# Out's weight combinations on another engine and in pieces, block fetches ahead of loads, x scaled one product later, last output on two queues

## The chip, the cores and the metric

The kernel runs on one core of one Trainium2 chip. The metric is the device time of one execution in microseconds (us), as a median over the runs that lie in the fast state. The kernel before takes 1222.24 us (1219.61 to 1223.46, three runs). "Faster" or "slower" needs a difference of over 2%.

Engine names in the profile: PE is TensorE's matmul side and PEld its weight loading, DVE is VectorE, ACT is ScalarE, POOL is GpSimd, SP is SyncE. A name with a "q" behind it (SPq, ACTq) is the engine's sequencer, which issues DMA transfers.

## The reference, cut to what matters

```python
# q, k, v: (8 batches, 8 heads, 576 positions, 64), fp32
scores = q @ k.T / sqrt(64) * Dmat[h]        # Dmat: gamma[h]**(i-j) for i >= j, else 0
attn = scores @ v                            # -> x: (4608 tokens, 512)
xn = x / sqrt(mean(x*x) + 1e-6) * rms_g
g, val = xn @ w_gate, xn @ w_val             # 512 -> 1536
out = (silu(g) * val) @ w_out                # 1536 -> 512
```

All is fp32.

## The kernel before

The 4608 tokens are cut into 12 blocks u of 384. Blocks 0 and 1 are computed with plain products. Blocks 2 to 11 use a scheme with 7 products of half-size quarters in place of 8, in the manner of Strassen. It needs sums of the quarters of the weights and of x.

- **Up stages.** Each block has six stages i = 0 to 5, alternately for the gate and for the value. A stage has seven products in the order x y z x w z w (these letters are the PSUM banks they write), of 8 matmuls and 1.30 us each.
- **Out.** Then come seven products xo zo wo yo xo zo wo of 24 matmuls and 3.90 us each. Product k reads a block of combined weights in slot k % 4 of the tile `w_out`. The seven blocks lie in DRAM (`w_blocks`, 768 KB each), because only four fit.
- **Attention slots.** Between stages stands the attention work for a later block: many small 64x64 matmuls, then transposes and scalings on DVE and ACT, then the loads for the next but one.

The combination of the weights for Out, which happens once, and its fetches:

```python
def keep(blk, t):
    nc.sync.dma_start(out=w_blocks[blk], in_=t)

def combine_out():
    a11, a12, a21, a22 = (quarter(r, c) for r in range(2) for c in range(2))
    for o, a, b, op in (
        (a22, a21, a22, ALU.add), (a21, a11, a21, ALU.subtract),
        (a11, a22, a11, ALU.subtract), (a12, a12, a11, ALU.subtract),
    ):
        nc.gpsimd.tensor_tensor(out=o, in0=a, in1=b, op=op)      # 128 x 6 x 256
    return (S1, a22), (S3, a21), (S2, a11), (S4, a12)

def fetch():
    nonlocal n_fetched
    if n_fetched < 7 * (NU - 2):
        nc.sync.dma_start(
            out=w_slots[:, n_fetched % 4], in_=w_blocks[ORDER[n_fetched % 7]])
        n_fetched += 1

def across(u):                                 # Out of block u
    ...
    def product(rhs, ps, start):
        k = 7 * (u - 2) + n_done
        ...                                    # 24 matmuls with w_slots[:, k % 4]
        fetch()                                # refills the slot just read
    ...
    def result(row, col, a, ps):
        ...                                    # add, transpose into o
        for d in range(2):
            for i in range(P // SQ):
                nc.sync.dma_start(out=out[...], in_=o[i * SQ : i * SQ + SQ, d])
```

The order of the work. `slot` is the attention work, `following` prepares the next slot and issues loads (13 of them) for the one after it, and `norm_2` scales the next block's x and forms the sums of its quarters (the four instructions `L412`):

```python
def following(j):
    if j + 1 < len(jobs):
        prepare(j + 1)                         # two DVE transposes, four ACT scalings
    if j + 2 < len(jobs):
        load_qk(j + 2)
        load_kv(j + 2)

SLOTS = (((0, 2, 4, 5), 5), ((5,), 9), ((1, 3, 5), 10))    # stages with a slot, by u % 3

def behind(u, i):
    at, n = SLOTS[u % 3]
    if i in at:
        j = u // 3 * 8 + n + at.index(i)
        slot(j)
        following(j)
    if u + 1 < NU and i >= 5:
        (norm_0, norm_1, norm_2)[i - 5](u + 1)

kept = start()                                 # blocks 0 and 1; ends with combine_out()
for u in range(2, NU):
    for i in range(2 * NG):
        for _ in up(u, i % 2, i // 2):
            pass
        if u == 2 and i == 2:
            for blk, t in kept:
                keep(blk, t)
            for _ in range(4):
                fetch()
        if i == 2 * NG - 1:
            rest = across(u)
            next(rest)
        behind(u, i)
    for i, _ in enumerate(rest):               # after each product of Out
        if i in (1, 3):
            behind(u, 6 + i // 2)
```

## Time and profile before

| | before |
|---|---|
| time, median of 3 runs | 1222.24 us |
| span of the profiled run | 1222.0 us |
| PE busy | 1150.0 us, 94% |
| DVE busy | 676.9 us, 55% |
| DMA fetches of weight blocks | 70 of 768 KB |

The waits view lists, for TensorE, what it stood waiting for. Its columns are engine, tile and line, what released the wait, then microseconds in total, the number of waits and the longest. For the kernel before, from 280 us to the end, beside the wait of xo:

```profile
PE y L432 <- DVE sums L412: 8.1, 1, 8.1
...
PE z L432 <- DVE sum L282: 4.0, 1, 4.0
PE ms L379 <- DVE sq L372: 1.4, 7, 0.2
PE wo L557 <- DVE h L568: 0.5, 2, 0.2
```

A single wait of 8.1 us and one of 4.0 stand beside small ones that recur. From 280 us on, such a list, with the half clock that follows some of the waits and the tail after the last matmul, is nearly the whole inventory of what a change to the order of the work can win.

### The profile page before, as it was taken

What the parts mean: (1) busy time and instruction counts of PE and PEld (TensorE: products, weight loads), DVE (VectorE), ACT (ScalarE), POOL (GpSimd) and SP (SyncE); (2) the same over time, 40 slices, a digit from 0 to 9 for tenths busy, and PEclk for the clock granted to TensorE, in tenths of its full rate; (3) what the DMA queues carried; (4) which work ended last, traced back from release to release, by engine and by line L of the source; (5) the groups of instructions that cost most, each with busy time, mean ns of one, the idle gap of its engine ahead of it and who ended that gap; (6) DMA issues with size and microseconds to landing.
All of it is one profiled execution on the core that took longest, in us unless ns stands there. A gap on an engine that the chain in (4) does not pass through costs nothing.

```text
span 1222.0 us, 24026 instructions
## 1 busy us (share of the span) xinstructions
PE 1150.0 (94%) x10184; PEld 1036.6 (85%) x10184; DVE 676.9 (55%) x1346; ACT 244.1 (20%) x468; POOL 59.7 (5%) x78
## 2 busy tenths in 40 slices
PE   4697899996999999999999999999999999999997
PEld 3555555444998999999998999999999999999997
DVE  3888871027565567446556557437557555436352
ACT  4454550010220121120120121120120120110110
POOL 0000004134000000000000000000000000000000
PEclk9798799997999999999999999999999999999999
DMA  8588431020386426306335526405345503404203
GB/s 220 120 207 206 125 119 52 18 64 14 73 246 180 104 44 181 98 1 177 84 62 150 134 40 162 121 1 151 97 76 148 137 2 105 103 1 143 65 4 101
DMA packets 302347, 126.28 MB, mean 103 GB/s; under 512 B 279328, under 2 KB 284832, under 8 KB 302240
## 3 DMA queue, kind: packets, MB, share of 16 engines
q1 hardware_dynamic: 293168, 105.70, 35.2%
q10 hardware_dynamic: 9072, 19.05, 4.8%
q8 instruction: 80, 1.31, 0.5%
q14 instruction: 27, 0.22, 0.1%
HBM read 109.75 MB, written 14.94 MB: 102 GB/s over the span
## 4 chain that ended last, share of the span: by engine, by line
PE 74%; DVE 9%; DMA 3%; SPq 1%; issue 1%; ACT 0%; DVEq 0%; POOL 0%; POOLq 0%
PE x L432 13%; PE z L432 13%; PE w L432 13%; PE y L432 6%; PE up L489 6%; PE wo L557 6%; PE out L503 5%; PE xo L557 4%; PE zo L557 4%; DMA w_out<-w_blocks 3%; DVE sum L282 1%; PE av L318 1%; DVE h L568 1%; PE yo L557 1%; DVE sums L412 1%; PE av L299 1%
## 5 line engine op out<-in xcount | busy, mean ns | idle before, releaser
L456 ACT COPY m<-x 128x384 f32<-128x384 f32 x60 | 28.7, 478 | 439.4 <-PE x L432 439.4
L432 PE MATMUL z<-x,w_gate 128*128 128x192 f32 x480 | 89.3, 330 | 4.0 <-DVE sum L282 4.0
L557 PE MATMUL xo<-h,w_out 128*128 128x192 f32 x480 | 84.3, 333 | 6.8 <-DMA w_out<-w_blocks 6.8
L557 PEld LDWEIGHTS xo<-h,w_out 128*128 128x128 f32 x480 | 79.5, 193 | 12.0 <-issue 10.9
L432 PE MATMUL x<-x,w_gate 128*128 128x192 f32 x480 | 89.3, 329 | 0.0
L432 PE MATMUL x<-x,w_val 128*128 128x192 f32 x480 | 88.8, 328 | 0.0
L432 PE MATMUL z<-x,w_val 128*128 128x192 f32 x480 | 87.8, 326 | 0.0
L432 PE MATMUL w<-sums,w_val 128*128 128x192 f32 x480 | 87.8, 326 | 0.0
L432 PE MATMUL w<-sums,w_gate 128*128 128x192 f32 x480 | 87.8, 326 | 0.0
L432 PEld LDWEIGHTS z<-x,w_gate 128*128 128x128 f32 x480 | 80.7, 192 | 4.5 <-DVE sum L282 4.5
L557 PE MATMUL wo<-h,w_out 128*128 128x192 f32 x480 | 82.3, 328 | 0.5 <-DVE h L568 0.5
L432 PEld LDWEIGHTS x<-x,w_gate 128*128 128x128 f32 x480 | 80.1, 192 | 0.5
L432 PEld LDWEIGHTS x<-x,w_val 128*128 128x128 f32 x480 | 79.2, 190 | 0.6
L432 PEld LDWEIGHTS w<-sums,w_val 128*128 128x128 f32 x480 | 79.7, 190 | 0.0
L432 PEld LDWEIGHTS w<-sums,w_gate 128*128 128x128 f32 x480 | 79.7, 190 | 0.0
L432 PEld LDWEIGHTS z<-x,w_val 128*128 128x128 f32 x480 | 79.6, 190 | 0.0
L557 PEld LDWEIGHTS wo<-h,w_out 128*128 128x128 f32 x480 | 77.9, 190 | 1.1 <-DVE h L568 1.1
L439 DVE TENSOR_TENSOR u<-m,y 128x384 f32<-128x384 f32 x60 | 32.6, 543 | 80.0 <-PE y L432 77.8
L439 DVE TENSOR_TENSOR h<-u,w 128x384 f32<-128x384 f32 x60 | 33.2, 554 | 78.2 <-PE w L432 78.2
L489 PE MATMUL up<-x,w_gate 128*128 128x384 f32 x192 | 67.7, 512 | 3.7 <-DVE x L401 1.8
L489 PEld LDWEIGHTS up<-x,w_gate 128*128 128x128 f32 x192 | 37.9, 200 | 32.6 <-issue 4.9
L489 PE MATMUL up<-x,w_val 128*128 128x384 f32 x192 | 65.0, 499 | 0.0
(120 smaller groups left out, 1759.9 us busy)
## 6 DMA issues: line engine op xcount, KB each, us to landing
w_out<-w_blocks SPq DMA_DIRECT2D x70, 768.0 KB, 4.9
k<-in_k_dram SPq DMA_DIRECT2D x64, 128.0 KB, 2.9
v<-in_v_dram SPq DMA_DIRECT2D x64, 128.0 KB, 2.9
qraw<-in_q_dram SPq DMA_DIRECT2D x112, 72.0 KB, 2.5
kraw<-in_k_dram SPq DMA_DIRECT2D x112, 72.0 KB, 2.6
out_dram<-o SPq DMA_DIRECT2D x320, 24.0 KB, 3.4
w_out<-in_moe_w_gate_dram ACTq DMA_DIRECT2D x6, 1024.0 KB, 6.3
w_blocks<-w_out SPq DMA_DIRECT2D x7, 768.0 KB, 5.7
```

Source lines behind the costliest of these rows:

```text
L282: nc.vector.scalar_tensor_tensor(out=t[:, c], in0=t[:, c - 1], scalar=gc[:, hp : hp + 1], in1=part, op0=ALU.mult, op1=ALU.add,)
L299: mm = nc.tensor.matmul(av[odd][side(e), i * L : i * L + L], lhsT=d["v"][side(odd), i, e] if c < NC - 1 else d["vt"][:, e], rhs=d["ret"][s ...
L318: mm = nc.tensor.matmul(av[odd][side(e), i * L : i * L + L], lhsT=d["sum"][side(e), c - 1], rhs=d["qT"][side(e), c * L : c * L + L], start ...
L412: nc.vector.tensor_tensor(out=o, in0=a, in1=b, op=ALU.subtract)
L432: nc.tensor.matmul(ps[:, i * HU : i * HU + HU], lhsT=w_up[m][:, 2 * blk + c, cut], rhs=t_of[u][blk][:, c], start=(start and i == c == 0), ...
L439: nc.vector.tensor_tensor(out=o, in0=a, in1=pairs_of(ps), op=ALU.add)
L456: nc.scalar.copy(out=s1, in_=pairs_of(x_))
L489: nc.tensor.matmul(ps[:, :U], lhsT=w_up[m][:, 4 * half + c, i * P : i * P + P], rhs=x_of[u][:, c], start=(c == 0), stop=(c == NHP - 1),)
L503: nc.tensor.matmul(ps[:, :DM], lhsT=h_of[u][:, f, s * P : s * P + P], rhs=w_out[:, f], start=(f == 0), stop=(f == NF - 1),)
L557: nc.tensor.matmul(ps[:, i * HU : i * HU + HU], lhsT=w_slots[:, k % 4, c, i * P : i * P + P], rhs=rhs[:, c], start=(start and i == c == 0) ...
L568: nc.vector.tensor_tensor(out=o, in0=a, in1=b, op=op)
```

## The change

The intent has three parts. Part 1: Out's weights are combined on VectorE in 24 pieces, one behind each of the first 24 products of block 2, so that GpSimd no longer holds up VectorE. Part 2: in Out, three fetches go out ahead of the loads of the last slot, the other four go out two each after stages 1 and 3 of the next block, and x is scaled one product of Out later. Part 3: half of the last block's output transfers go to ScalarE's queue.

```diff
@@ -351,12 +351,18 @@
         if rest and j > 0:
             carried(j - 1)
 
-    def following(j):
+    def prepare_next(j):
         if j + 1 < len(jobs):
             prepare(j + 1)
+
+    def load_next(j):
         if j + 2 < len(jobs):
             load_qk(j + 2)
             load_kv(j + 2)
+
+    def following(j):
+        prepare_next(j)
+        load_next(j)
 
 
 
@@ -525,12 +531,17 @@
     def combine_out():
 
         a11, a12, a21, a22 = (quarter(r, c) for r in range(2) for c in range(2))
-        for o, a, b, op in (
-            (a22, a21, a22, ALU.add), (a21, a11, a21, ALU.subtract),
-            (a11, a22, a11, ALU.subtract), (a12, a12, a11, ALU.subtract),
-        ):
-            nc.gpsimd.tensor_tensor(out=o, in0=a, in1=b, op=op)
-        return (S1, a22), (S3, a21), (S2, a11), (S4, a12)
+        for c in range(NH):
+            for o, a, b, op in (
+                (a22, a21, a22, ALU.add), (a21, a11, a21, ALU.subtract),
+                (a11, a22, a11, ALU.subtract), (a12, a12, a11, ALU.subtract),
+            ):
+                nc.vector.tensor_tensor(out=o[:, c], in0=a[:, c], in1=b[:, c], op=op)
+                yield
+        for blk, t in ((S1, a22), (S3, a21), (S2, a11), (S4, a12)):
+            keep(blk, t)
+        for _ in range(4):
+            fetch()
 
     def fetch():
         nonlocal n_fetched
@@ -559,7 +570,8 @@
                         lhsT=w_slots[:, k % 4, c, i * P : i * P + P], rhs=rhs[:, c],
                         start=(start and i == c == 0), stop=False, skip_group_check=True,
                     )
-            fetch()
+            if n_done < 3:
+                fetch()
 
         def add(o, a, ps):
             nc.vector.tensor_tensor(out=o, in0=a, in1=ps[:, :U], op=ALU.add)
@@ -579,7 +591,8 @@
                 for i in range(P // SQ):
                     c0 = row * DH + d * P + i * SQ
                     t0 = u * U + col * HU
-                    nc.sync.dma_start(
+                    queue = nc.scalar if u == NU - 1 and d else nc.sync
+                    queue.dma_start(
                         out=out[t0 : t0 + HU, c0 : c0 + SQ].rearrange("(t c) r -> c t r", c=SQ),
                         in_=o[i * SQ : i * SQ + SQ, d],
                     )
@@ -818,7 +831,6 @@
                 following(8)
         slot(9)
         following(9)
-        return combine_out()
 
 
 
@@ -829,28 +841,34 @@
         if i in at:
             j = u // 3 * 8 + n + at.index(i)
             slot(j)
-            following(j)
+            prepare_next(j)
+            if i < 2 * NG - 1:
+                load_next(j)
         if u + 1 < NU and i >= 5:
             (norm_0, norm_1, norm_2)[i - 5](u + 1)
 
     with tc.manual_schedule():
-        kept = start()
+        start()
         for u in range(2, NU):
+            made = combine_out() if u == 2 else iter(())
             for i in range(2 * NG):
                 for _ in up(u, i % 2, i // 2):
-                    pass
-                if u == 2 and i == 2:
-                    for blk, t in kept:
-                        keep(blk, t)
-                    for _ in range(4):
-                        fetch()
+                    next(made, None)
+                if u > 2 and i in (1, 3):
+                    fetch()
+                    fetch()
                 if i == 2 * NG - 1:
                     rest = across(u)
                     next(rest)
                 behind(u, i)
             for i, _ in enumerate(rest):
-                if i in (1, 3):
-                    behind(u, 6 + i // 2)
+                if i == 1:
+                    behind(u, 6)
+                elif i == 2 and 2 * NG - 1 in SLOTS[u % 3][0]:
+                    at, n = SLOTS[u % 3]
+                    load_next(u // 3 * 8 + n + len(at) - 1)
+                elif i == 4:
+                    behind(u, 7)
 
 
 # ---- launch: one core; inputs and outputs as the reference has them ----
```

## The prediction

> **What bounds the kernel now.** I read the page's busy times first, then the waits of TensorE, then the timeline where a wait was long. The page:
>
> ```profile
> PE 1150.0 (94%) x10184; PEld 1036.6 (85%) x10184; DVE 676.9 (55%) x1346; ACT 244.1 (20%) x468; POOL 59.7 (5%) x78
> ...
> PE 74%; DVE 9%; DMA 3%; SPq 1%; issue 1%; ACT 0%; DVEq 0%; POOL 0%; POOLq 0%
> ```
>
> TensorE (PE) is busy 94% of the span and carries 74% of the chain that ended last. The change removes no matmul, so it can only win the time in which PE stands still or runs at a lower clock, and only where nothing else would hold it there. I listed every PE gap above 0.25 us from the timeline. After 150 us there are few: two near 290 us, six ahead of xo (the fifth product of Out), and the tail after the last matmul. The first pair, in the timeline:
>
> ```profile
> 283.83 14.52 POOL L532 TENSOR_TENSOR w_out<-w_out 128x1536 f32<-128x1536 f32 x4
> 285.11 2.58 DVE L412 TENSOR_TENSOR sums<-x 128x384 f32<-128x384 f32 x1
> 287.73 3.65 DVE L412 TENSOR_TENSOR x<-x 128x384 f32<-128x384 f32 x1
> 291.42 3.66 DVE L412 TENSOR_TENSOR sums<-x 128x384 f32<-128x384 f32 x1
> 295.11 3.66 DVE L412 TENSOR_TENSOR sums<-x,sums 128x384 f32<-128x384 f32 x1
> 295.13 2.93 PE L432 MATMUL y<-sums,w_gate 128*128 128x192 f32 x8 [8.08 <-DVE sums L412]
> 302.04 2.93 PE L432 MATMUL z<-x,w_gate 128*128 128x192 f32 x8 [3.98 <-DVE sum L282]
> 306.77 1.46 PE L432 MATMUL w<-sums,w_gate 128*128 128x192 f32 x8
> ...
> 386.31 0.56 DVE L412 TENSOR_TENSOR sums<-x 128x384 f32<-128x384 f32 x1
> ```
>
> The same VectorE (DVE) instruction takes 0.56 us one block later. While GpSimd (POOL) combines Out's weights, in four instructions of 14.52 / 4 = 3.63 us, each of the four L412 ends one POOL instruction later than the one before. PE first waits 8.08 us for the third of them, then 3.98 us for the bank that DVE empties after the fourth. Both times PE then runs at half clock: 8 matmuls take 2.93 us instead of 1.46.
>
> The other waits, from the waits view, the timeline of the first Out block, and the end:
>
> ```profile
> PE xo L557 <- DMA w_out<-w_blocks: 6.8, 7, 2.3
> ...
> 370.77 1.95 SPq L142 DMA_DIRECT2D qraw<-in_q_dram  x4
> 379.25 2.85 SPq L538 DMA_DIRECT2D w_out<-w_blocks  x4
> 384.67 5.82 PE L557 MATMUL xo<-h,w_out 128*128 128x192 f32 x24 [2.27 <-DMA w_out<-w_blocks]
> ...
> 1203.97 15.77 SPq L582 DMA_DIRECT2D out_dram<-o  x32
> 1209.13 4.06 PE L557 MATMUL wo<-h,w_out 128*128 128x192 f32 x24
> 1213.82 0.58 DVE L576 STREAM_TRANSPOSE o<-c 128x384 f32<-128x384 f32 x1
> ```
>
> The fetches of Out's weight blocks stand in SP's queue behind 13 loads for attention (370.77 to 379.25), although the slot that the first fetch overwrites has been free since the first product ended near 369 us. At the end SP issues 32 output transfers back to back until 1219.74, while the last result has been ready since 1214.40.
>
> **What the Trainium skill says.** "SBUF — State Buffer", "Who interferes with whom": a DVE instruction with two SBUF inputs and a GpSimd instruction that reads SBUF share a read interface; the later one blocks fully until the other ends. The trace agrees (3.66 us against 0.56, in step with 3.63). It follows that the same sums on DVE itself cannot block DVE in this way. "TensorE: Matmul & The Clock Gate", "What's actually happening": the clock is halved after an idle window of about 3.4 us, and the windows run freely. The trace goes further: an idle of 2.27 us before xo sufficed once (24 matmul starts span 5.49 us instead of 3.81), one of 1.87 us at 662 us did not (3.81). "DMA: Bandwidth & Descriptors", "Issuing engines are not separate DMA queues": a second issuing engine saves only the time that the sequencer takes to issue. At the tail that time is exactly the cost: 32 issues of about 0.485 us each fill SP's 15.77 us. At the start of this trace SP and ScalarE (ACT) do issue side by side, at 0.39 to 0.50 us each.
>
> **Part 1: Out's combinations on DVE.** Removed: 14.52 us of POOL. Added: 24 DVE instructions of 128x256, one after each of the first 24 products. From 128x384 (0.56 us) and 128x1152 (1.35 us) the slope is 0.79 / 768, so about 1.03 ns an element, and 128x256 costs 0.43 us, 0.46 with the gap between instructions: 11 us of DVE in all.
> The replay near 285 us: the four L412 now follow each other at 0.59 us and end at 287.45. y needs the third (286.85), so it starts right behind x at 287.06 and ends at 288.4. The attention work that stood behind them on DVE took 298.70 to 301.98, 3.28 us, until it freed z's bank; it now ends near 290.73. So z starts at 290.75 and a gap of 2.35 us stays. The third product behind it, w, starts at 290.75 + 2 x 1.30 = 293.35 instead of 306.77 to 306.93: 13.5 us won if PE stays at full clock. The 2.35 us gap resembles the 2.27 us one that cost 1.68 us of clock. I assume that an idle of at least 1.95 us within one window (3.41 us, the page's figure) halves the clock; over all phases of the window that is (1.06 + 0.80) / 3.41 = 55%. Expected cost 0.9 us.
> The DVE pieces: a gate stage has 5 DVE additions of 0.58 and 7 pieces of 0.46, 6.1 us in PE's 9.1; a val stage has 9 additions, 8.4 in 9.1. It fits, but an attention slot adds 5.4 us. Replaying two stages: z's second product waits for u4 some 0.3 us and w's second one 0.15, at the first stage and again at the third, and the slot between delays z by 0.4: 1.3 us, less where the clock is low anyway.
> Part 1: 13.5 - 0.9 - 1.1 = 11.5 us.
>
> **Part 2: block fetches first, x scaled later.** Three fetches now stand ahead of the loads, and the other four of the next block go out during its up products. A fetch lands about 4.9 us after issue (the page's issues table), and between the end of product k and product k+4 lie three products of 3.90 us, so all PE gaps before xo go: 2.27 + 0.57 + 0.55 + 1.87 + 1.08 + 0.29 = 6.6 us, and 1.7 us of half clock at the first. The loads move back by some 7 us; their data is used a stage (over 9 us) and a slot later, so I see no new wait. Scaling x after xo gives DVE's subtraction for the last product room: it saves two waits of 0.23 us. With T the start of xo: DVE has the subtraction done near T+5.9, x scaled at T+8.1, the sums at T+10.5; the last product starts at T+8.6 and the next block at T+12.5. No wait.
> Part 2: 6.6 + 1.7 + 0.5 = 8.8 us.
>
> **Part 3: last output on two queues.** PE ends at 1213.2 and the result stands at 1214.40 as before, relative to PE. With 4 issues left on each queue the last is out at 1214.40 + 4 x 0.485 = 1216.3 instead of 1219.74; the landing (1.6 us) stays. 3.4 us, if ACT and SP issue side by side.
>
> Sum: 11.5 + 8.8 + 3.4 = 23.7 us, 1222.2 - 23.7 = 1198.5. I move that by 1 us to 1199.5, because each part assumes that nothing takes the wait's place.
>
> **Rivals.** First, DVE becomes the bound in the first six stages: the pieces come in program order ahead of additions that PE waits for, and every slot leaves a debt. For it: a val stage is 92% full. Against: the debt is 5.4 us against 3 us of slack in the next gate stage plus 2.6 us of the slot's own PE time. If I have its size wrong, part 1 shrinks to 7 or 8 us: 1203. Second, the moved fetches or loads only shift the wait: outputs get stuck behind 13 loads, their three buffers fill, and DVE waits at its fourth transpose, or attention waits for late loads. For it: SP issues some 22 us an Out block. Against: the next attention use is over 20 us away in blocks that keep one slot. It would halve part 2: 1203. Third, issuing is shared: two queues each at half rate leave the tail as it is: 1202. All three: about 1210. On the good side, the gap at 288 us may not halve the clock and the pieces may hide wholly: 1196.
>
> **Range and chances.** 1194 to 1207 holds the single failures and the noise of the runs before (1219.6 to 1223.5). Faster by over 2% means under 1197.8, within 2 us of my sum: 0.34. Slower by 2% would need a new wait of 48 us: 0.02. Within 2%: 0.64.
>
> **What would show it.** L412 at 0.56 us each, no PE wait over 3 us near 290 us, and z starting near 290.7; the waits of xo on w_out gone from the waits view; SP's last stretch of outputs half as many and last issue some 2 us after the last transpose. Wrong would be: DVE pieces as releasers of PE waits between 290 and 320 us above 3 us in sum, new waits of PE or DVE on output or attention transfers, or ACT issuing at double the duration.

## The result and the profile after

The changed kernel takes 1202.14 us (1198.87 to 1202.94, four runs) against 1221.65 (1219.61 to 1223.46, four runs) for the kernel before on the same chip. The ratio is 0.9836 with a 95% interval of 0.9811 to 0.986, which is within 2%. The page of the changed kernel:

```profile
span 1201.0 us, 24041 instructions
...
PE 1147.4 (96%) x10184; PEld 1036.7 (86%) x10184; DVE 674.6 (56%) x1370; ACT 244.3 (20%) x468; POOL 44.9 (4%) x74
...
PE 82%; DVE 13%; issue 2%; ACT 1%; DMA 1%; SPq 0%; POOL 0%; DVEq 0%; ACTq 0%; POOLq 0%
```

POOL lost its four instructions and DVE gained 24. PE does the same 10184 matmuls in a span that is 21.0 us shorter. The waits of TensorE after, from 280 us on:

```profile
PE z L438 <- DVE sum L282: 2.2, 1, 2.2
PE av L318 <- issue: 2.0, 1, 2.0
PE ms L385 <- DVE sq L378: 1.5, 7, 0.2
PE av L318 <- POOL tick L307: 0.3, 1, 0.3
```

The wait on `sums` and all waits of xo are gone, and z waits 2.2 us instead of 4.0. One line is new: av, released by "issue", which means that the profile shows nothing that it waited for. The timeline at the start of block 2 (lines picked from it: start, duration, engine, line, instruction, and in brackets the idle before it) shows part 1:

```profile
286.67 0.56 DVE L418 TENSOR_TENSOR sums<-x 128x384 f32<-128x384 f32 x1
287.26 0.56 DVE L418 TENSOR_TENSOR x<-x 128x384 f32<-128x384 f32 x1
287.85 0.56 DVE L418 TENSOR_TENSOR sums<-x 128x384 f32<-128x384 f32 x1
288.45 0.56 DVE L418 TENSOR_TENSOR sums<-x,sums 128x384 f32<-128x384 f32 x1
288.47 1.57 PE L438 MATMUL y<-sums,w_gate 128*128 128x192 f32 x8
292.27 2.93 PE L438 MATMUL z<-x,w_gate 128*128 128x192 f32 x8 [2.24 <-DVE sum L282]
294.35 0.38 DVE L539 TENSOR_TENSOR w_out<-w_out 128x256 f32<-128x256 f32 x1
296.54 1.46 PE L438 MATMUL w<-sums,w_gate 128*128 128x192 f32 x8
```

The four instructions that took 2.58 to 3.66 us take 0.56 each, y starts at once, and z waits only for attention work on DVE. After the 2.24 us the clock is halved from 292.06 to 295.47, so eight matmuls of z take 2.93 us. A piece of the combination costs 0.42 us (median of the 24; the one shown took 0.38).

The new stop, in the timeline of block 9, with SP's fetches that went before it:

```profile
955.18 2.39 SPq L549 DMA_DIRECT2D w_out<-w_blocks  x4
...
964.06 0.91 PE L318 MATMUL av<-qT,sum 64*64 64x64 f32 x24
966.99 0.45 PE L318 MATMUL av<-qT,sum 64*64 64x64 f32 x8 [2.02 <-issue]
967.37 2.44 PE L438 MATMUL x<-x,w_val 128*128 128x192 f32 x8
```

It falls into the middle of 32 equal small matmuls of the slot behind stage 2. The matmuls behind it run at half clock (967.9 to 971.3). The windows view of the same stretch says what else was busy; its columns are the stretch, its length, busy time of PE, PEld, DVE, ACT and POOL, the clock granted to TensorE (1.00 is full speed), share of the DMA engines' time, and GB/s:

```profile
955.00:962.00 7.00, 7.00 (x45) 7.00 (x44) 2.22 (x4) 1.40 (x4) 0.00 (x0) 1.00 0.94 333
962.00:964.00 2.00, 2.00 (x109) 1.77 (x109) 0.56 (x1) 1.22 (x4) 0.09 (x1) 1.00 1.05 436
964.00:965.00 1.00, 0.97 (x42) 0.89 (x35) 0.68 (x2) 0.92 (x4) 0.00 (x0) 1.00 0.55 213
965.00:966.00 1.00, 0.00 (x0) 0.00 (x0) 0.91 (x4) 0.00 (x0) 0.00 (x0) 1.00 0.04 6
```

The 16 DMA engines are full for the nine microseconds in which the four fetches (3 MB) move, and PE stands still just when they have become idle. The second reading is PE's rate: 218 instructions (109 matmuls and 109 weight loads) in 2 us of the slot, against 89 in 7 us of the stage before it.

The tail (lines picked from the timeline):

```profile
1186.37 12.24 SPq L595 DMA_DIRECT2D out_dram<-o  x16
1186.38 12.31 ACTq L595 DMA_DIRECT2D out_dram<-o  x16
1191.53 4.06 PE L568 MATMUL wo<-h,w_out 128*128 128x192 f32 x24
1196.22 0.58 DVE L588 STREAM_TRANSPOSE o<-c 128x384 f32<-128x384 f32 x1
```

SP and ACT issue 16 transfers each side by side, at some 0.45 us each. They are done at 1198.61 and 1198.69, the later one 1.89 us after the last transpose ended (1196.80); before, it was 5.34 us (1219.74 and 1214.40).

**Where the 21 us went.** I compared the start of the same products in the two traces. Such start-to-start times don't depend on the modelled ends of the matmuls.

| stretch | predicted | traces |
|---|---|---|
| up to block 2's first product (the program is the same there) | 0 | +1.6 |
| part 1: first product x to w, two products behind z (21.28 to 9.50 us) | -12.6 | -11.8 |
| part 1: pieces delay later products of block 2 | +1.1 | 0.0 |
| part 2: waits of xo and wo, blocks 2 to 10 | -8.8 | -11.0 |
| part 3: after the last product | -3.4 | -3.4 |
| new: stop in block 9 and half clock behind it | "1 us" | +3.9 |
| sum (spans: -21.0) | -22.7 | -20.7 |

The first line is scatter: over the traces of all kernels that keep this part of the program, that product starts between 285.5 and 287.8 us. The last is the finding to be explained: 2.24 us of stop, start to start, and 0.83 and 0.85 us on two products at half clock.

### The profile page after: what moved, and what is told of

Same layout as the page of the kernel before. It is cut to its first block, busy times and chain, and to the rows that moved or that the text cites. A ratio compares the mean times of both kernels' runs of the same rounds, so it can differ in the third digit from the quotient of the medians.

```text
span 1201.0 us, 24041 instructions
## 1 busy us (share of the span) xinstructions
PE 1147.4 (96%) x10184; PEld 1036.7 (86%) x10184; DVE 674.6 (56%) x1370; ACT 244.3 (20%) x468; POOL 44.9 (4%) x74
## 3 DMA queue, kind: packets, MB, share of 16 engines
q8 instruction: 80, 1.31, 0.5%
## 4 chain that ended last, share of the span: by engine, by line
PE 82%; DVE 13%; issue 2%; ACT 1%; DMA 1%; SPq 0%; POOL 0%; DVEq 0%; ACTq 0%; POOLq 0%
PE x L438 13%; PE z L438 13%; PE w L438 13%; PE up L495 7%; PE wo L568 7%; PE y L438 6%; PE out L509 5%; PE xo L568 4%; PE zo L568 4%; PE yo L568 3%; DVE sum L282 2%; PE av L318 1%; DVE sq L378 1%; DVE ret L270 1%; DVE x L333 1%
## 5 line engine op out<-in xcount | busy, mean ns | idle before, releaser
L438 PEld LDWEIGHTS w<-sums,w_gate 128*128 128x128 f32 x480 | 79.6, 190 | 0.0
L438 PEld LDWEIGHTS w<-sums,w_val 128*128 128x128 f32 x480 | 79.6, 190 | 0.0
L438 PEld LDWEIGHTS z<-x,w_val 128*128 128x128 f32 x480 | 79.6, 190 | 0.0
L457 ACT ACTIVATE h<-h 128x384 f32<-128x384 f32 x90 | 47.0, 523 | 88.6 <-DVE h L445 88.6
```

The source lines that it names most:

```text
L438: nc.tensor.matmul(ps[:, i * HU : i * HU + HU], lhsT=w_up[m][:, 2 * blk + c, cut], rhs=t_of[u][blk][:, c], start=(start and i == c == 0), ...
L457: nc.scalar.activation(out=o, in_=c, func=AF.Silu)
```

## The experiments

My theory of the new stop, T: the four fetches of block 9, which now go out back to back, fill the DMA engines; TensorE's own instructions come in by DMA too and come late; and a slot uses instructions up so fast that PE runs dry. Rival one: such stops happen in some executions by chance, whatever the kernel. Rival two: it comes from the queue (SP's, late and behind the loads), not from the burst. The expectations also test the terms of my sum: each part alone, x's scaling, and the pieces. In their text my theory and its rivals carry names or letters of their own; each says beside it what it expects. "Before" medians of the three groups of runs were 1223.19, 1223.00 and 1222.14 us. All results were correct.

### The changed kernel again

No edit.

> The changed kernel unaltered, to see how steady it is. In its first trace TensorE stops 2.0 us at 965 us, in the attention slot of block 9, with nothing that it waits for, and runs 3.4 us at half clock after it; together 3.9 us. It begins as four block fetches (3 MB) that SP issued back to back at 955 us run out, and a 16 KB packet of the instruction queue starts at that moment (964.8). Theory A: the stop is TensorE waiting for instructions that were stuck behind the burst; it depends on the phase, so some executions have it and some don't: times from 1198.5 to 1203, and a trace without the stop should show a span near 1197. Theory B: the stop belongs to the place in the program and is in every execution: all times within 1202 +/- 1.5, and the trace has the stop in the same slot.

Measured: 1198.93 us (1197.48 to 1200.64, five rounds), ratio 0.9803 (0.9784 to 0.9823), on the 2% line. The stop is there again at the same instruction, 1.43 us long from 963.58 to 965.01, without half clock. The wait of z is 2.24 us as before, this time without half clock either. So the two traces of this one kernel differ by 3.7 us in span, and two places account for it within half a microsecond: 2.3 us at the stop and the half clock behind it (3.9 against 1.6, start to start) and 1.7 us at z (z to w: 4.27 us, against 2 x 1.30 at full clock). Rival one, chance, is weakened: the stop came twice out of twice.

### Part 1 alone

The kernel before with the combination on VectorE in pieces:

```diff
-            nc.gpsimd.tensor_tensor(out=o, in0=a, in1=b, op=op)
+        for c in range(NH):  # around the four operations
+                nc.vector.tensor_tensor(out=o[:, c], in0=a[:, c], in1=b[:, c], op=op)
+                yield        # one after each product of block 2
```

> The kernel before, with the combinations of Out's weights on VectorE in 24 pieces and nothing else. If the three parts add up: 11.8 us faster than before, about 1210 (the step from the first product of block 2 to the third in the two traces). If part 1 only moves time into the first wait for block fetches in block 2: 8 us or less. If the pieces cost TensorE what I predicted (1.1 us), they show as TensorE waits on VectorE between 295 and 345 us; in the trace of the changed kernel I find none, so I expect none here.

Measured: 1208.85 us (1207.10 to 1209.81), ratio 0.9882 (0.9863 to 0.9902), so 14.4 us of 1222.5. From block 2's first product to w, two products behind z, the trace takes 7.93 us against 21.28 before. That is 13.4 us less, and 1.6 more than the first trace of the full change had won there, because here the 2.24 us before z halved no clock. Beyond that the first xo of block 2 waited 0.74 us instead of 2.27 and stayed at full clock, which won 3.2 more, and in block 5 a longer wait with a half clock behind it lost 2.1. So 13.4 is part 1's own gain in this trace, and the rest is what a moved phase did to waits of part 2. No PE wait names DVE's pieces. There is no stop in block 9.

### Part 2 alone

The kernel before with part 2's lines of the diff.

> The changed kernel with the combinations back on GpSimd in four whole instructions and the last output on one queue: part 2 alone. The two traces give 11.0 us for it (4.2 in block 2, 0.4 to 2.1 in each other block), less a stop of about 3.9 us in block 9 if that comes with the new place of the fetches. Theory A (stop made by the burst of fetches): 1211 where the execution has no stop, 1215 where it has; the stop can be in the trace. Theory B (stop has nothing to do with part 2): no stop here, 1211 throughout.

Measured: 1215.44 us (1213.81 to 1215.85), ratio 0.9932 (0.9913 to 0.9951), so 8.3 us. All waits of xo are gone. The stop is there, 1.43 us, in the slot of block 9. It comes with part 2, and neither with part 1 nor with the kernel before.

### Part 3 alone

```diff
-                    nc.sync.dma_start(
+                    queue = nc.scalar if u == NU - 1 and d else nc.sync
+                    queue.dma_start(
```

> The kernel before with only the last output on two queues. If issuing is each queue's own, the last issue comes 3.4 us earlier after the last transpose: 3.4 us faster, ratio 0.997. If the two queues share the issuing and each goes at half the rate: no change, with issues of ScalarE and SP of near 0.9 us instead of 0.44.

Measured: 1219.44 us (1217.26 to 1222.49), ratio 0.9978 (0.9964 to 0.9993): 2.7 us, with 3.4 inside the interval. In the trace the end lies 3.40 us nearer to the last product. Both queues issue at their full rate: median 0.446 us on SP and 0.452 us on ACT. There is no stop in block 9. The three parts alone sum to 14.4 + 8.3 + 2.7 = 25.4 us; together they gave 20.0 us in the first measurement (0.0164 x 1221.65) and 24.1 in the second (0.0197 x 1223.2).

### x scaled early again

```diff
-                elif i == 4:
+                elif i == 3:
                     behind(u, 7)
```

> The changed kernel with x of the next block scaled where it was before, one product earlier. I had given the later place 0.5 us (two waits of 0.23). Theory A (worth more than I thought once the fetches are early): VectorE's 4.5 us of scaling and sums then stand ahead of the subtraction that the last product needs, in all nine blocks and not in two, because no wait for a fetch hides it any more; each costs the 0.39 us that blocks 9 and 10 showed: 3 to 4 us slower than e0_again, about 1202.5, with TensorE waits of wo on VectorE's h in nine blocks. Theory B (it hardly matters): within 1 us of e0_again.

Measured: 1203.48 us (1202.94 to 1206.37), ratio 0.985 (0.9817 to 0.9883). The waits view of this kernel has a new first line:

```profile
PE wo L568 <- DVE h L580: 2.4, 9, 0.5
```

The last product of Out waits in nine blocks, for DVE's subtraction that stands behind the scaling of x. Start to start each costs about 0.40 us (once 0.68), 3.9 us in all. In the kernel before this wait stood in two blocks only (0.5 us): in the other seven the fetch wait ahead of xo had given DVE the time. So scaling later is worth about 4 us once the fetch waits are gone, not the 0.5 that I read from the waits before.

### Whole combinations on VectorE

```diff
-        for c in range(NH):
-            ... nc.vector.tensor_tensor(out=o[:, c], in0=a[:, c], in1=b[:, c], op=op)
-                yield
+            nc.vector.tensor_tensor(out=o, in0=a, in1=b, op=op)      # 128 x 1536
+            for _ in range(6):
+                yield
```

> The changed kernel with Out's combinations on VectorE in four whole instructions of 128x1536, one after every sixth product, instead of 24 pieces. About 1.03 ns an element makes 1.75 us each. Theory A (pieces matter because VectorE is in order and TensorE waits behind each instruction): TensorE waits on VectorE between 290 and 325 us, 1 to 2 us each at two or three of the four: 2 to 4 us slower than e0_again. Theory B (only the engine matters, since two sources on VectorE cannot be blocked by GpSimd once GpSimd does nothing): within 1 us of e0_again.

Measured: 1200.10 us (1199.61 to 1201.08), ratio 0.9815 (0.9789 to 0.9841). This ran in other rounds than the changed kernel itself. Kernels are compared only within the same rounds. Two waits that the changed kernel doesn't have, both of z, cost 0.96 and 0.54 us start to start:

```profile
PE z L438 <- DVE sum L282: 2.6, 2, 2.2
...
PE z L438 <- DVE u L445: 0.8, 1, 0.8
```

The engine alone carries nearly all of part 1. Cutting into pieces is worth about 1.5 us in this trace.

### Fetches spread

The four fetches between one block's Out and the next block's go to ScalarE's queue, one each after stages 1 to 4.

```diff
-    def fetch():
+    def fetch(queue=nc.sync):
...
-                if u > 2 and i in (1, 3):
-                    fetch()
-                    fetch()
+                if u > 2 and i in (1, 2, 3, 4):
+                    fetch(nc.scalar)
```

> The changed kernel with the four block fetches that it issues during the up products taken from SP's queue to ScalarE's, one after each of the products' stages 1 to 4, so that ScalarE's own order spreads them by some 9 us instead of SP sending four together in blocks 9 to 11. Theory A: no burst, so no stop in block 9's slot in any execution: about 1198, 4 us better than the changed kernel where that has the stop, and as good as its best run. Theory B: the stop stays at its place, time as e0_again. A third way: ScalarE's issues delay its activations and TensorE waits on ScalarE: slower than e0_again by several us.

Measured: 1196.09 us (1195.68 to 1197.09), ratio 0.9781 (0.9763 to 0.9799): faster by over 2%. The stop is gone. After 150 us only z's 2.24 us stand over 0.28 us. This fits T, and rival two as well, because queue and burst changed together. The next three runs separate them.

### A burst on the other queue, early

The spread kernel, but block 9's four fetches go out together on ScalarE's queue after stage 1.

```diff
+                if u == 9 and i == 1:
+                    for _ in range(4):
+                        fetch(nc.scalar)
```

> e3_spread, with one thing changed: in block 9 ScalarE issues its four fetches together after stage 1 instead of one after each stage. It tells the burst from the queue, since in e3_spread the fetches had also left SP. If the burst delays TensorE's instructions: the stop of 1.4 to 2 us is back in block 9's slot after stage 2, with the instruction packet that starts at 960.2 in e3_spread some 2 us later, and nowhere else; about 2 us slower than e3_spread. If what mattered was the queue (SP): no stop, time as e3_spread.

Measured: 1196.92 us (1195.75 to 1197.99, three rounds), ratio 0.9788. No stop. My expectation failed, and the trace says why: ScalarE's queue has no loads to wait behind, so the burst began at 944.80 and was over at about 957, before the slot. The run did not test what it was made for. It shows something else, though. The loads that the burst had held back kept the DMA engines busy up to the slot, and still PE did not stop:

```profile
953.00:960.00 7.00, 7.00 (x45) 7.00 (x44) 2.37 (x5) 1.28 (x3) 0.00 (x0) 1.00 0.94 174
960.00:964.00 4.00, 4.00 (x146) 3.77 (x146) 1.62 (x4) 2.04 (x6) 0.09 (x1) 1.00 0.48 107
```

In the trace of the changed kernel run again, the first of these stretches has a share of 0.93 at 306 GB/s. So a high DMA share alone does not make the stop.

### A burst on the other queue, in time

The spread kernel, but block 9's four fetches go out on ScalarE's queue inside stage 2, after its first product.

```diff
+                    if u == 9 and i == 2 and n == 0:
+                        for _ in range(4):
+                            fetch(nc.scalar)
```

> e9_burst put the burst at 944.8, 9 us earlier than in the changed kernel, because ScalarE does not stand behind the loads as SP does; it had run out before the instruction packet at 961.0, and no stop came, so that run did not tell the burst from the queue. Here ScalarE issues the four fetches of block 9 within stage 2, after its first product, near 953.8, where SP issues them in e0_again. If the burst at that moment is the cause: the stop of 1.4 to 2 us is back, about 2 us slower than e3_spread (1198), with the instruction packet near 962.7 instead of 960.2. If the queue is what matters: no stop, 1196.

Measured: 1201.24 us (1197.85 to 1201.88, three rounds), ratio 0.9823 (0.9808 to 0.9838). The stop is back, on a queue that has nothing to do with SP. In its timeline:

```profile
965.10 0.45 PE L318 MATMUL av<-qT,sum 64*64 64x64 f32 x7 [2.40 <-issue]
...
965.47 2.76 PE L438 MATMUL x<-x,w_val 128*128 128x192 f32 x8
```

With the half clock behind it, it brings back about what spreading had won. The windows view of the same stretch, here and then in the spread kernel:

```profile
953.50:963.00 9.50, 9.20 (x175) 8.89 (x174) 3.77 (x8) 2.06 (x4) 0.09 (x1) 1.00 1.00 365
```

```profile
953.50:963.00 9.50, 9.50 (x176) 9.28 (x176) 3.18 (x6) 3.14 (x8) 0.09 (x1) 1.00 0.21 47
```

A DMA share of 1.00 goes with the stop, one of 0.21 without; with the early burst, though, 0.94 went without it too. Here the four large fetches make most of it (365 GB/s over the stretch).

### A burst on the old queue, early

The changed kernel, but the four fetches go out on SP's queue after stage 0, ahead of the loads.

```diff
-                if u > 2 and i in (1, 3):
-                    fetch()
-                    fetch()
+                if u > 2 and i == 0:
+                    for _ in range(4):
+                        fetch()
```

> The other half of the same test: the fetches stay on SP, in one burst of four, but are issued in the order after stage 0, ahead of the loads of that slot. In block 9 the burst then begins near 943 and has run out by 955, before the instruction packet near 961. If it is the moment of the burst: no stop in block 9, and about 1196 to 1197, as e3_spread, if no other packet of instructions is hit. If it is the queue or the place in the program: the stop stays, 1199.

Measured: 1196.91 us (1195.87 to 1197.66), ratio 0.9793 (0.978 to 0.9805). The burst is there on SP's queue, from 941.94, and there is no stop. So the moment of the burst decides, and neither the queue nor the burst by itself. Rival two falls.

### What the instruction packets show

The page lists two queues of kind "instruction". The first has the same line in the kernel before and after:

```profile
q8 instruction: 80, 1.31, 0.5%
```

It moved 80 packets, which at 1.31 MB are 16 KB each. The Trainium skill, "Runtime: NRT & Kernel Launch", "Instruction fetch mechanics", says that an engine's instructions are refilled in blocks of 16 KiB, 256 instructions each, and that the sequencer fetches the next page by a DMA queue of its own while the current one runs. PE has 10184 matmuls and 10184 weight loads on the page, and 20368 / 256 is 79.6: 80 blocks. So q8 is TensorE's instruction stream; in the spread kernel 255 of PE's recorded instructions lie between two of its packets on average. I then counted PE's recorded instructions up to each packet of q8 and up to the stop. The packet in question is the 67th; "due" is the start of the 17,076th instruction, the first to start after it went out in the spread kernel:

```
kernel                 due      packet starts, ends   PE: last before, then 17,346th
changed                961.85   964.77  965.73        964.75   966.99   stop 2.02
changed again          960.46   962.68  963.65        963.37   965.01   stop 1.43
burst on ACT in time   959.68   962.50  963.70        962.48   965.10   stop 2.40
spread                 960.28   960.15  961.02        963.03   963.03   none
burst on ACT early     961.17   961.05  962.13        963.92   963.92   none
SP early               960.83   960.16  961.53        963.47   963.47   none
before                 982.96   982.27  983.63        985.39   985.44   none
```

(The last columns hold starts of instructions; the stop is counted from the end of the last matmul. "Due" is good to about 0.7 us, as the last two rows show.) In these three traces, and in all four others with a stop, it stands at one place in the program, before the 17,346th recorded instruction. In the three, PE goes on 1.26 to 1.40 us after the packet's end. Where the packet goes out when due, PE has 2.75 us for the 270 instructions up to that place in the spread kernel (960.28 to 963.03). The packet and what follows it took 2.2 to 2.6 us. So a slot leaves about half a microsecond or less by this count, which is itself no better than its due time, and a packet 2.2 to 2.9 us after its due time can't be hidden. In an up stage, at 16 instructions in 1.30 us, 256 last 20.8 us, and the same delay costs nothing. It fits that four fetches in a row at 489.53 and at 763.46 in the changed kernel stop nothing. Over all 14 traces, the stop is in the seven where four fetches run into this slot (the changed kernel twice, part 2 alone, x early, whole combinations, normalisation earlier, the burst in time) and in none of the other seven. In the first seven the packet starts 1.7 to 2.9 us after its due time, in the others 0.1 to 0.9 us before it.

What stays inferred is how the burst holds the packet up: the trace shows the large fetches and the late packet side by side, and not where the packet stood meanwhile. Two details stay open. With the early burst the engines were as full around the due time (share 1.01 from 960 to 961, 0.83 to 962), and the packet left on time; the traffic then was the held-back loads, in packets of 128 and 256 bytes, and not the fetches, in packets of 6 KB. And in two of the three rows with a stop the packet starts just 0.02 us after the last instruction before the stop has started, as if it had been asked for only then; in the third it starts 0.69 us before that one. No run here decides what holds the packet.

### Normalisation of block 2 earlier

The wait of z that is left hangs on DVE, which does block 2's normalisation, attention work and sums in a row. Here the three norm steps of block 2 come before `down(u, s)` instead of after it.

```diff
             for s in range(NS):
-                down(u, s)
                 if u == 0:
                     (norm_0, norm_1, norm_2)[s](2)
+                down(u, s)
```

> The changed kernel with the three steps of block 2's norm each one plain output tile earlier, so that VectorE scales x and makes the sums while TensorE still works on block 0's last tile, and the attention slot's VectorE work follows the slot directly. If the 2.24 us gap before z at 290 us is VectorE's order of work alone, it goes, and with it the half clock that follows it in some executions (1.7 us): 2.3 to 4 us faster than e0_again, about 1196. If the gap comes from somewhere else (a bank, a load), z still waits there and the time stays.

Measured: 1196.29 us (1195.86 to 1197.39), ratio 0.9784 (0.9758 to 0.981). z's wait is gone, and the stop of block 9 (1.37 us) heads what is left in the waits view beside the small waits known from before:

```profile
PE av L318 <- issue: 1.4, 1, 1.4
```

### Both mends

The changed kernel with the fetches spread and the normalisation earlier, both edits as shown above.

> The version that should beat both: e3_spread's fetches and e7_norm_early's order together. Each removes another pause (the stop in block 9, 1.6 to 3.9 us; the gap before z, 2.2 us and at times 1.7 of half clock), so if they add up: 4.5 to 6 us under e0_again, about 1193.5, with no TensorE pause over 0.5 us after 150 us. If they share something: 1196, as each alone.

Measured: 1194.29 us (1193.71 to 1194.99), ratio 0.9772 (0.976 to 0.9785). This beats both kernels, and is faster than the kernel before by over 2%. Its list of waits from 280 us on is down to the last two lines of the changed kernel's list, ms (1.5 us in seven waits) and av behind POOL's tick (0.3 us).

The gains of the two mends don't depend on each other: one takes a wait out at 290 us, the other at 965 us, and PE has nothing else to wait for in between.

## Why the prediction was right or wrong

The predicted 1199.5 us and the range of 1194 to 1207 hold both measurements of the change, 1202.14 and 1198.93, and the class that I gave the best chance, within 2%, came true. The second measurement's interval of ratios reaches across the line, as the chance of 0.34 said it might.

**Part 1, right.** The replay of DVE's queue put z at 290.75 us with a gap of 2.35. The trace has it at 292.27 with 2.24; block 2 began 1.55 us later in that trace, so on the old scale z is at 290.72. The 13.5 us at full clock is also what came: 11.8 plus the 1.67 that half clock took from z, and 13.4 in the trace of part 1 alone, where the clock stayed full. The term for the pieces, 1.1 us, was too high: they delayed nothing. A piece takes 0.42 us in the median where I had reckoned 0.43, so the cost was right and the waits behind it were not: no PE wait in the first six stages names DVE's additions, though my replay had such waits at three places.

The claim that the halving of the clock is a matter of phase held: the same 2.24 us halved the clock in the first trace of the change and did not in the second. The traces allow more than that. In each, the half-clock spells begin and end on a grid of 3.413 us, but for the one that the end of the trace cuts off (292.06 and 967.90 in the first trace are 198 steps apart). I counted PE's idle time in each step of that grid, in all 14 traces, from 280 us to 15 us before the end. Each of the eight steps at full clock with 2.02 us or more of idle was followed by half clock, and none with 1.87 us or less was. Of the 2.24 us, 2.03 fell into one step in the first trace and at most 1.78 in the second. The 1.95 us that the prediction assumed lies between.

The Trainium skill's statement in "SBUF — State Buffer", "Who interferes with whom", that the two engines block each other on the read interface agrees again, with 0.56 us in place of 3.66 once GpSimd is out of the way.

**Part 2, right in kind, undersized.** All waits of xo went, as argued from the 4.9 us of a fetch against three products of 3.90. The gain is 11.0 us against 8.8, for a reason of method: the gaps I summed run from a modelled end of the matmul before, and start-to-start times show about 0.2 us more for each (0.81 against 0.57 in block 3, 2.11 against 1.87 in block 5). The term "0.5 for x" was the worst sized: it counted only the waits visible before, and the run with early scaling shows about 4. The fetch waits had masked it.

**Part 3, right.** 3.4 us predicted, 3.41 measured in the changed kernel and 3.40 alone. The rival of shared issuing falls with 0.45 us an issue on both queues. It agrees with "DMA: Bandwidth & Descriptors", "Issuing engines are not separate DMA queues": what was won is issuing time alone.

**The step that failed** is "so I see no new wait" in part 2, and with it the single microsecond that I set aside because "each part assumes that nothing takes the wait's place". I had followed the loads that moved back by 7 us to the instructions that read them, and that reading was right: no wait on a load appeared. I had not asked when the four fetches would go out, and what else is on the DMA engines then. In block 9 they stood behind the loads that SP began to issue only at 948.10, and left together at 955.18: these loads are the last of the kernel, so none stood between the first pair and the second. That cost 1.6 to 3.9 us, at an instruction with no wait in the program. This and the mis-sized terms are of opposite signs, which is why the sum was nearer than its parts.

**Rivals.** DVE did not become the bound (no wait on the pieces), no output or load wait appeared, and issuing wasn't shared. None of the three named the wait that came.

## What to carry to other kernels

Before moving transfers, ask not only when their data is needed but what else will be on the DMA engines then: here a burst of large transfers went with a late packet of an engine's own instructions, and the profile showed it as a stop released by "issue" in a stretch of many short instructions. Spread large transfers, or put the burst in a stretch of long instructions. And a wait that is small before can be small because another wait covers it: size it by undoing that part alone, with times taken from start to start.

## What the Trainium skill lacked or had wrong

- "Runtime: NRT & Kernel Launch", "Instruction fetch mechanics", calls the cost of crossing a block boundary "mostly hidden". In these traces it is, with one exception that the page doesn't name: where four fetches of 768 KB ran into an attention slot (DMA share 0.94 to 1.05 in the first trace), a block's packet came 1.7 to 2.9 us late in seven traces, and TensorE stood 1.4 to 2.4 us.
- The same section explains that fetching hides because an engine issues more slowly than it is filled. In the attention slot of block 9 TensorE started 270 instructions in 2.75 us, and a packet took 2.2 to 2.6 us from its start to the first instruction behind it, so the margin was about half a microsecond or less.
- "TensorE: Matmul & The Clock Gate", "What's actually happening", halves the clock after an idle window of about 3.4 us. Here 2.02 us of idle within one step of 3.413 us sufficed, eight times out of eight from there up to 3.41, and 1.87 or less never did; the half clock behind the stop lasted one step (967.9 to 971.3).
